# Attention and gated MLP on one core: weights loaded ahead of later mask rows and transposes, the second pair's VectorE work interleaved, the last output row in two column parts

## Chip, cores, metric

One core of one Trainium2 chip. The metric is the device time of one execution in microseconds (us); runs of a kernel before and after the change were taken on the same chip, in rounds.

## The reference

Bucketed attention (a query sees only keys of the same 6-bit hash bucket), then a gated MLP with a gated residual:

```python
q, k, v: (4, 8, 768, 64) fp32       # batch, heads, rows, head dim
proj: (64, 6); w_gate, w_val: (512, 1536); w_out: (1536, 512); w_res: (512, 512)

bucket(t) = sum_j 2^j * ((t @ proj)[..., j] > 0)
scores    = where(bucket(q) == bucket(k), q k^T / 8, -1e9)
attn      = softmax(scores) v                     # -> x: (3072, 512)
g         = x @ w_gate
ffn       = (gelu(g) * (x @ w_val)) @ w_out
out       = x + sigmoid(x @ w_res) * ffn          # fp32
```

## The kernel before

Heads are worked in pairs, 16 in all, four pairs to a batch. A pair is split into chunks, and every chunk is a **slot** of a schedule: its scores (TensorE), its exponential (ScalarE), the tasks that `at(slot, ...)` hung there, some matmuls of the MLP of the batch before, and the value matmuls of an earlier chunk. `base(p)` is the first slot of pair p; pair 0 has 12 slots, every later one 9. Four slots into a new batch the whole gate and value stage of the batch before is run (`gate_val`, 192 matmuls; no scores come in between, only the value matmuls that are still outstanding). In batch 0 there is no MLP to mix in.

In the traces here each engine takes its own instructions in program order (SyncE, SP, issues pair 5's load at 33.25 us, behind the two transposes hung ahead of it at 28.37). So the order in which tasks are hung is the order in which SP issues transfers and VectorE (DVE) makes copies. What the argument touches:

```python
    def load(p, what, ...):                 # q, k (sides 0, 1) or v (2) of pair p: nc.sync.dma_start
    def load_w():                           # 512 KB of a weight into one of NWS = 4 staging tiles, nc.sync
    def cast_w():                           # GpSimd: staging tile -> bf16 weight; frees the staging tile
    def transpose_dma(x):                   # nc.sync: nat -> aug
    def move_second(x):                     # GpSimd: rows 64..127 of aug -> second
    def mask_rows(p, engines):              # 4 small transfers: bucket rows into aug and second
    def blocks(x, ...):                     # DVE: 32x32 transposes of the raw load, for the hash
    def hash_half(p, dh, bank=(tp_ps, "tp")):
        ...
        for j, (x, c0, n) in enumerate(q4): # four column strips of TensorE, one for each operand
            nc.tensor.matmul(hs[32 * j:32 * j + 32], projw[:, dh, :],
                             t32[x][:, c0:c0 + n, dh, :], start=(dh == 0), stop=(dh == 1),
                             tile_position=(0, 32 * j), skip_group_check=True)
    # ... cut ...
    at(base(1) + 3, mask_rows, 2)
    for side in range(2):
        at(base(1) + 3, transpose_dma, (3, side))
    at(base(1) + 3, load, 3, (2,))
    at(base(1) + 4, load, 5, (0, 1))        # (cut: in program order behind the lines above)
    # ... cut ...
    for side in range(2):
        at(base(3) + 4, transpose_dma, (5, side))
    for i in range(NWS):
        at(base(2) + 1, load_w)             # first four weight loads
    # ... cut: load 5 (2,) ...
    at(base(3) + 4, load, 6, (0, 1))
    at(base(3) + 5, load, 7, (0, 1))
    # ... cut: load 6 (2,) ...
    for i in range(NWS):
        at(base(2) + 5 + i, cast_w)
        at(base(3) + 4, load_w)             # second four
        at(base(3) + 5 + i, cast_w)
    # ... cut: the end ...
    flush()                                 # the last value matmuls
    mlp_matmuls(HELD[-1])                   # HELD[-1] = 15 output matmuls kept for this place
    x_transpose(NPAIR - 1)
    gate_val(B - 1, flush)
    for _ in project(B - 1, ((row_ps, "row"), (av_ps, "av")), nc.vector):
        pass
```

## Time and profile before

| | before |
|---|---|
| median of its first three timed runs | 359.07 us (358.67 to 359.46) |
| the profiled run / its span on the core | 361.94 / 360.2 us |
| TensorE busy | 344.8 us of 360.2 |
| first matmul of the first gate stage | 55.81 us |
| first score after that stage | 89.97 us |

The profiled run is 2.9 us slower than the median of the timed ones. The lines of the profile stand in the prediction.

### The profile page before, as it was taken

How to read it: one execution, taken by the hardware profiler on the slowest of the kernel's cores; microseconds unless marked ns; L12 is line 12 of the kernel's file. 1: busy time of each engine (PE TensorE's matmuls, PEld its weight loads, DVE VectorE, ACT ScalarE, POOL GpSimd, SP SyncE). 2: the span in 40 equal slices, each digit the busy share in tenths (PEclk: the TensorE clock that was granted, in tenths of full speed). 3: DMA queues.
4: the chain of work that ended last, by engine and by line, in shares of the span. 5: the costliest groups of instructions: out<-in, count | busy, mean ns of one | idle time of the engine just before them, and what ended most of it. 6: DMA issues, size and time to landing. Idle time of an engine off the chain costs nothing.

```text
span 360.2 us, 7593 instructions
## 1 busy us (share of the span) xinstructions
PE 344.8 (96%) x3094; PEld 201.4 (56%) x3094; DVE 152.9 (42%) x229; ACT 211.7 (59%) x238; POOL 153.9 (43%) x194
## 2 busy tenths in 40 slices
PE   8899889799999999999999999999999999999994
PEld 4556366466465565566555566656555655666442
DVE  6884433243553346343452545434452024434243
ACT  5799696223778787323778788332778874232210
POOL 6696760976658579200048769300037222000000
PEclk9999999999999999999999999999999999999998
DMA  7748879999633583740002773510002220000012
GB/s 239 230 152 118 259 218 265 309 324 306 173 132 104 124 270 101 177 159 0 2 32 73 169 256 104 116 44 3 0 2 62 82 53 34 24 2 1 31 63 83
DMA packets 52574, 44.06 MB, mean 122 GB/s; under 512 B 31640, under 2 KB 44348, under 8 KB 52540
## 3 DMA queue, kind: packets, MB, share of 16 engines
q1 hardware_dynamic: 52396, 43.56, 41.9%
q8 instruction: 24, 0.39, 0.5%
q14 instruction: 10, 0.08, 0.1%
q0 software_dynamic: 64, 0.02, 0.0%
q10 hardware_dynamic: 80, 0.00, 0.0%
HBM read 29.36 MB, written 6.29 MB: 99 GB/s over the span
## 4 chain that ended last, share of the span: by engine, by line
PE 74%; POOL 10%; issue 5%; DMA 4%; DVE 3%; SPq 2%; ACT 1%; POOLq 0%; DVEq 0%; ACTq 0%
PE sp L457 31%; PE fps L487 15%; PE sp L435 11%; PE av L406 7%; PE rps L477 5%; PE hs L274 3%; POOL ldv L332 2%; POOL second L208 2%; DMA x_sb<-x_tok 2%; DMA ld<-in_k_dram 1%; POOL va L326 1%; SPq L203 1%; POOL wg L177 1%; POOL wv L177 1%; PE spr L287 1%
## 5 line engine op out<-in xcount | busy, mean ns | idle before, releaser
L439 ACT ACTIVATE e<-sp 128x1024 bf16<-128x1024 f32 (+1 forms) x147 | 144.7, 1007 | 33.9 <-PE sp L435 31.0
L463 ACT ACTIVATE gt<-sp 128x768 bf16<-128x768 f32 x48 | 38.9, 811 | 86.8 <-PE sp L457 86.8
L464 DVE SCALAR_TENSOR_TENSOR hh<-gt,sp 128x768 bf16<-128x768 bf16 x48 | 45.8, 954 | 83.8 <-PE sp L457 83.8
L487 PE MATMUL fps<-wo,hh 128*128 128x512 bf16 x288 | 76.4, 378 | 0.7 <-DVE o L492 0.7
L457 PE MATMUL sp<-x_sb,wg 128*128 128x512 bf16 (+1 forms) x384 | 71.1, 326 | 2.0 <-POOL wg L177 1.5
L457 PE MATMUL sp<-x_sb,wv 128*128 128x512 bf16 (+1 forms) x384 | 70.4, 326 | 0.3 <-POOL wv L177 0.3
L406 PEld LDWEIGHTS <-e 128*128 128x128 bf16 x1152 | 49.8, 97 | 31.8 <-issue 9.3
L406 PE MATMUL av<-va,e 128*128 128x65 bf16 x1152 | 56.1, 193 | 0.9 <-ACT e L439 0.7
L435 PE MATMUL sp<-aug,aug 71*128 71x512 bf16 x192 | 54.3, 326 | 1.9 <-ACT e L439 1.1
L435 PE MATMUL sp<-second,second 128*128 128x512 bf16 x192 | 54.3, 325 | 0.1
L457 PEld LDWEIGHTS <-wg 128*128 128x128 bf16 x384 | 37.3, 98 | 26.9 <-POOL wg L177 1.9
L457 PEld LDWEIGHTS <-wv 128*128 128x128 bf16 x384 | 37.4, 98 | 25.7 <-POOL wv L177 1.1
L494 POOL TENSOR_TENSOR o<-o,x_tok 128x512 f32<-128x512 f32 x18 | 20.8, 1156 | 56.1 <-DVE o L492 52.8
L487 PEld LDWEIGHTS <-hh 128*128 128x128 bf16 x288 | 27.6, 97 | 26.2
L383 POOL TENSOR_TENSOR x_tok<-total,rec 128x768 bf16<-128x768 f32 x9 | 13.3, 1473 | 49.2 <-DVE rec L382 49.2
L492 DVE SCALAR_TENSOR_TENSOR o<-th,fps 128x512 f32<-128x512 f32 x24 | 16.3, 681 | 39.5 <-PE fps L487 35.7
L208 POOL COPY second<-aug 64x768 bf16<-64x768 bf16 x30 | 24.4, 826 | 17.8 <-DMA aug<-nat 15.3
L237 DVE STREAM_TRANSPOSE t<-ld 128x768 f32<-128x768 f32 (+1 forms) x34 | 29.5, 907 | 2.7 <-DMA ld<-in_q_dram 2.3
L477 PE MATMUL rps<-wr,x_sb 128*128 128x512 bf16 x96 | 24.6, 379 | 0.0
L480 ACT ACTIVATE th<-rps 128x512 f32<-128x512 f32 x24 | 14.3, 596 | 17.4 <-PE rps L477 13.9
L435 PEld LDWEIGHTS <-second 128*128 128x128 bf16 x192 | 18.5, 98 | 5.1 <-issue 2.2
L294 DVE CAST bits<-spr 128x512 bf16<-128x512 f32 (+1 forms) x24 | 15.6, 656 | 8.9 <-PE spr L287 8.8
(67 smaller groups left out, 247.8 us busy)
## 6 DMA issues: line engine op xcount, KB each, us to landing
ldv<-in_v_dram SPq DMA_DIRECT2D x16, 384.0 KB
out_dram<-o SPq DMA_DIRECT2D x24, 256.0 KB
ld<-in_q_dram SPq DMA_DIRECT2D x15, 384.0 KB
ld<-in_k_dram SPq DMA_DIRECT2D x15, 384.0 KB
ws<-in_moe_w_gate_dram SPq DMA_DIRECT2D x6, 512.0 KB
ws<-in_moe_w_val_dram SPq DMA_DIRECT2D x6, 512.0 KB
ws<-in_moe_w_out_dram SPq DMA_DIRECT2D x6, 512.0 KB
ws<-in_moe_w_res_dram SPq DMA_DIRECT2D x2, 512.0 KB
```

The costliest lines, as they stand in the source:

```text
L208: eng.tensor_copy(second[x[0] % NM][x[1]][D:P], aug[x][D:P])
L237: nc.vector.transpose(t32[x][:, c0:c1].rearrange("p c h n -> p (c h n)"), raw[x][:, c0:c1].rearrange("p c d -> p (c d)"))
L406: nc.tensor.matmul(o[:, qt0 + i, :], e[:, off + i * P:off + (i + 1) * P], va[:, hi, jt, 0:D + 1], start=(hi not in begun), stop=(jt == T - ...
L435: nc.tensor.matmul(sp[:, off:off + nq * P], ks[0:n, jt, :], qs[0:n, qt0:qt0 + nq, :], start=True, stop=True)
L439: nc.scalar.activation(e[:, 0:n], sp[:, 0:n], AF.Exp, scale=float(ALPHA))
L457: nc.tensor.matmul(sp[:, c0:c1], w[:, kk, bass.ts(m, P)], xs[:, kk, c0:c1], start=(kk == 0), stop=(kk == KM - 1))
L463: nc.scalar.activation(gt, sp[:, 0:S], AF.Gelu)
L464: nc.vector.scalar_tensor_tensor(hh[:, m, :], gt, 0.5, ps[1][:, 0:S], op0=ALU.mult, op1=ALU.mult)
L477: nc.tensor.matmul(rps, x_sb[b][:, kk, t, :], wr[:, kk, :], start=(kk == 0), stop=(kk == KM - 1))
L487: nc.tensor.matmul(fps, hh[:, m, bass.ts(t, P)], wo[:, m, :], start=(m == 0), stop=(m == KF - 1))
L492: nc.vector.scalar_tensor_tensor(o, th, 1.0, fps, op0=ALU.add, op1=ALU.mult)
L494: last.tensor_add(o3, o3, x_tok[b][:, :, t, :])
```

## The change

It moves work; apart from twelve more matmuls, two more DVE steps and one more store in the last row, it neither adds nor drops any. Six parts, cut to their core:

```diff
 # 1 start
+    cast((0, 0), nc.scalar, H0)            # ahead of the copies of the projection
...
-    cast((0, 0), nc.scalar, H0)
-        at(1 + side, blocks, (1, side))
     at(2, spread_in_place, (0, 1), (ROW, TP))
+    at(2, blocks, (1, 0))
...  at(4 + side, transposed, (1, side), nc.vector)
+        if side == 0:
+            at(4, blocks, (1, 1))
-        at(4, hash_half, 1, dh, ROW)
+        at(5, hash_half, 1, dh, ROW)       # its first spread: slot 6 -> 7
-        at(7, blocks, (2, side))
+        at(6 + side, blocks, (2, side))
 # 2 load of pair 5
+    at(9, load, 5, (0, 1))
-    at(base(1) + 4, load, 5, (0, 1))
 # 3 second four weight loads now lead slot base(3)+4; behind them
+        at(base(3) + 5, transpose_dma, (5, side))      # was +4, ahead of them
+    at(base(3) + 6, load, 6, (0, 1))                   # was +4, ahead of them
+    at(base(3) + 7, load, 7, (0, 1))                   # was +5
+    at(base(3) + 7, load, 6, (2,))                     # was +6
+    at(base(3) + 8, ...) move_second 5, values_prep 5, mask_rows 5   # were +6, +6, +7
 # 4 seam
-    HELD = [0] + [12] * (B - 2) + [15]
+    HELD = [0] + [12] * (B - 2) + [19]
+    flush(1)
+    mlp_matmuls(4)
     flush()
 # 5 tail, in project(): the last row of the last batch in columns 0..383 and 384..511
+            parts = ((0, KM - 1), (KM - 1, KM)) if t == T - 1 and len(pools) > 1 else ((0, KM),)
+            for i, (k0, k1) in enumerate(parts):  # matmuls, DVE steps and store of each part
 # 6 mask rows of a later pair
-        at(s0 + 15, mask_rows, p + 1)
+        at(s0 + 16, mask_rows, p + 1)
```

The intent: the holes at the start, where the exponentials pace the kernel, are to close, the weights are to be there when the first gate stage wants them, and the last steps are to overlap.

More of the change, by code (lines that the diff above doesn't have):

```diff
@@ L483, in project @@
                 nc.sync.dma_start(*store)
-            ps, tag = pools[t % len(pools)]
-            fps = ps.tile([P, DMODEL], FP32, tag=tag, name="fps")
-            for m in range(KF):
-                nc.tensor.matmul(fps, hh[:, m, bass.ts(t, P)], wo[:, m, :],
-                                 start=(m == 0), stop=(m == KF - 1))
-                if m < KF - 1:
-                    yield 1
-            o = o_pool.tile([P, DMODEL], FP32, tag="o", name="o")
-            nc.vector.scalar_tensor_tensor(o, th, 1.0, fps, op0=ALU.add, op1=ALU.mult)
-            o3 = o.rearrange("p (k n) -> p k n", k=KM)
-            last.tensor_add(o3, o3, x_tok[b][:, :, t, :])
-            store = (out_t[b, t], o)
-            yield 1
+            o = o_pool.tile([P, DMODEL], FP32, tag="o", name="o")
+            parts = ((0, KM - 1), (KM - 1, KM)) if t == T - 1 and len(pools) > 1 else ((0, KM),)
+            for i, (k0, k1) in enumerate(parts):
+                cs = slice(k0 * P, k1 * P)
+                ps, tag = pools[(t + i) % len(pools)]
+                fps = ps.tile([P, (k1 - k0) * P], FP32, tag=tag, name="fps")
+                for m in range(KF):
+                    nc.tensor.matmul(fps, hh[:, m, bass.ts(t, P)], wo[:, m, cs],
+                                     start=(m == 0), stop=(m == KF - 1))
+                    if m < KF - 1:
+                        yield 1
+                if store and i:
+                    nc.sync.dma_start(*store)
+                nc.vector.scalar_tensor_tensor(o[:, cs], th[:, cs], 1.0, fps,
+                                               op0=ALU.add, op1=ALU.mult)
+                o3 = o[:, cs].rearrange("p (k n) -> p k n", k=k1 - k0)
+                last.tensor_add(o3, o3, x_tok[b][:, k0:k1, t, :])
+                store = (out_t[b, t][:, cs], o[:, cs])
+                yield 1
         nc.sync.dma_start(*store)
@@ L582 @@
     at(1, transposed_head, (0, 1), 1, nc.vector)
-    for side in range(2):
-        at(1 + side, blocks, (1, side))
     at(2, spread_in_place, (0, 1), (ROW, TP))
+    at(2, blocks, (1, 0))
     for side in range(2):
@@ L591 @@
         at(4 + side, transposed, (1, side), nc.vector)
+        if side == 0:
+            at(4, blocks, (1, 1))
         at(5 + side, move_second, (1, side))
     for dh in range(2):
-        at(4, hash_half, 1, dh, ROW)
-    at(6, spread, 1, 0, 4, ROW)
+        at(5, hash_half, 1, dh, ROW)
+    at(7, spread, 1, 0, 4, ROW)
     at(7, spread, 1, 4, T, TP)
@@ L630 @@
         at(base(1) + 7, cast, (5, side))
-        at(base(3) + 6, move_second, (5, side))
         for i in range(2):
@@ L637 @@
     at(base(3) + 3, mask_rows, 4)
-    at(base(3) + 7, mask_rows, 5)
     at(base(2) + 3, values_prep, 4)
-    at(base(3) + 6, values_prep, 5)
     at(base(2), load, 4, (2,))
@@ L643 @@
         at(base(2), transpose_dma, (4, side))
-        at(base(3) + 4, transpose_dma, (5, side))
         at(base(2) + 3, move_second, (4, side))
@@ L648 @@
     at(base(2) + 6, load, 5, (2,))
-    at(base(3) + 4, load, 6, (0, 1))
-    at(base(3) + 5, load, 7, (0, 1))
-    at(base(3) + 6, load, 6, (2,))
     for i in range(NWS):
@@ L655 @@
         at(base(3) + 5 + i, cast_w)
+    for side in range(2):
+        at(base(3) + 5, transpose_dma, (5, side))
+    at(base(3) + 6, load, 6, (0, 1))
+    at(base(3) + 7, load, 7, (0, 1))
+    at(base(3) + 7, load, 6, (2,))
+    for side in range(2):
+        at(base(3) + 8, move_second, (5, side))
+    at(base(3) + 8, values_prep, 5)
+    at(base(3) + 8, mask_rows, 5)
     for p in range(6, NPAIR, 2):
```

## The prediction

> **What bounds the kernel now.** I read the busy tenths first, then the stretches, then each engine in order of time where TensorE (PE) or ScalarE (ACT) stops, then the queue of SyncE (SP).
>
> ```profile
> PE   8899889799999999999999999999999999999994
> ACT  5799696223778787323778788332778874232210
> ```
>
> One slice is 9.0 us. PE is full from slice 9 on, up to the last slice. So only three places can give time: the start, up to about 71 us, the seam before the last gate stage (about 300 us), and the tail. The stretches say the same:
>
> ```profile
> 30.00:40.00 10.00, 7.92 (x104) 4.80 (x102) 5.76 (x8) 8.61 (x10) 4.95 (x10) 1.00 0.99 194
> 60.00:71.00 11.00, 9.29 (x56) 5.03 (x53) 3.00 (x4) 3.24 (x4) 8.27 (x10) 1.00 0.95 316
> 174.00:225.00 51.00, 51.00 (x542) 29.62 (x540) 23.67 (x35) 41.18 (x44) 32.03 (x37) 1.00 0.40 112
> ```
>
> Columns: length, then busy time of PE, weight loads, VectorE (DVE), ACT, GpSimd (POOL), granted clock, DMA share, GB/s. At 174 to 225 PE has no hole: nothing moved there is worth anything. Batch 0 has no matrix work of the second half to mix in, so there the exponentials set the pace (0.77 us each in pair 0, 0.95 us in the later pairs) and a hole in ACT is lost time. From 8.96 us on, ACT has these:
>
> ```profile
> 15.56 4.62 ACT L439 ACTIVATE e<-sp 128x768 bf16<-128x768 f32 x6 [1.73 <-PE sp L435]
> 41.94 1.02 ACT L439 ACTIVATE e<-sp 128x1024 bf16<-128x1024 f32 x1 [2.97 <-PE sp L435]
> ```
>
> Behind the second stands this chain on PE, DVE and SP:
>
> ```profile
> 38.64 0.85 PE L274 MATMUL hs<-t,projw 128*32 128x384 f32 x6 [0.86 <-DVE x_sb L393]
> 37.16 0.98 DVE L237 STREAM_TRANSPOSE t<-ld 128x768 f32<-128x768 f32 x1 [1.87 <-DMA ld<-in_q_dram]
> 38.84 0.98 DVE L237 STREAM_TRANSPOSE t<-ld 128x768 f32<-128x768 f32 x1 [0.26 <-DMA ld<-in_k_dram]
> 28.37 4.20 SPq L203 DMA_TRANSPOSE aug<-nat  x2
> 33.25 0.46 SPq L90 DMA_DIRECT2D ld<-in_q_dram  x1
> ```
>
> The load of pair 5 goes out at 33.25, behind mask rows and two transposes; its block transposes on DVE wait 1.87 us; the copy to x_sb stands behind them; the hash matmuls, which need that copy's buffer and those blocks, wait; the scores behind the hash wait; ACT starves.
>
> The weights come next. The gate stage starts at 55.81 and stalls at its fifth column block:
>
> ```profile
> 69.14 0.82 PE L457 MATMUL sp<-x_sb,wg 128*128 128x512 bf16 x4 [1.50 <-POOL wg L177]
> 70.12 0.82 PE L457 MATMUL sp<-x_sb,wv 128*128 128x512 bf16 x4 [0.16 <-POOL wv L177]
> 71.11 0.82 PE L457 MATMUL sp<-x_sb,wv 128*128 128x512 bf16 x4 [0.16 <-POOL wv L177]
> 62.37 1.04 POOL L177 CAST wg<-ws 128x1024 bf16<-128x1024 f32 x1 [11.12 <-DMA ws<-in_moe_w_gate_dram]
> ```
>
> POOL stood idle 11.12 us for weights that SP issued only at 55.77. At the seam and at the tail:
>
> ```profile
> 300.01 0.42 PE L406 MATMUL av<-va,e 128*128 128x65 bf16 x8 [0.69 <-ACT e L439]
> 355.67 0.69 DVE L492 SCALAR_TENSOR_TENSOR o<-th,fps 128x512 f32<-128x512 f32 x1 [2.04 <-PE fps L487]
> 356.39 0.69 DVE L494 TENSOR_TENSOR o<-o,x_tok 128x512 f32<-128x512 f32 x1
> ```
>
> **What the Trainium skill says.** "DMA: Bandwidth & Descriptors", section "Anatomy of one DMA — SWDGE (gpsimd) path", says that a semaphore wait happens on the issuing sequencer before dispatch, not in the DMA engines. So one waiting transfer holds all behind it on SP; the trace agrees (pair 5's load behind the 4.20 us of transposes). It also gives some 2 us fixed per DMA; the mask rows of 10.5 KB land 1.7 to 2.1 us after issue. "TensorE: Matmul & The Clock Gate", section "Architectural detail: the array is 16× 32×32, not 1× 128×128", calls VectorE and ScalarE strict FIFO and lets PE pull only weight loads ahead; the holes above show that in-order blocking. The same page, "Wait — 56ns, not 53.3ns?", gives N / 2.4 GHz + 2.5 ns per streamed matmul: 216 ns for 512 columns, and the chain of work has 12 of them in 2.59 us, 216 ns each.
>
> **The change part by part.**
>
> 1. Start. ACT casts the first query half before it copies the projection. The half is there at 3.35 (DVE reads it then), so the cast ends at about 3.9 instead of 4.73; but the warm-up holds PE until 4.58, so the transposes start 0.2 us earlier. Then DVE: the two mask copies of head (0,1) now come before pair 1's block transposes (1.84 us), and the second of these and the hash go to slots 4 and 5. I replayed the order with the measured durations: mask copies 10.8 to 11.9, blocks (1,0) to 12.8, copy out to 13.4, blocks (1,1) to 14.35, hash on PE 14.37 to 15.15, scores of slot 6 at 15.35. ACT: slot 5 ends at 14.4, slot 6 starts at 15.85, where before slot 6 started at 16.33. So the 1.73 us hole isn't closed but comes one exponential later and shrinks to some 1.4. Pair 1's mask rows leave at about 17.85 (17.71 before), land near 20.9, and hold its first scores about there: I count **-0.4 us**.
>
> 2. Pair 5's load moves from slot 16 to slot 9, right behind pair 4's (SP at about 21). It is in memory long before 35 us, so both DVE waits go (1.87 + 0.26) and x_sb is copied before the hash asks. What stays is the hash itself, 0.78 us a half on PE between scores, plus av 0.24: a hole of about 0.45 us. 2.97 - 0.45 = **-2.5 us**.
>
> 3. Weights. The second four loads move ahead of pair 5's transposes (2.57 us), of pair 6's and 7's loads, and of pair 5's mask rows. They need buffers that POOL's first casts free; POOL no longer waits 1.69 + 0.75 us for pair 5's cast, so I have these casts done at 49 (51.25 before), the loads out at 47 to 50 instead of 55.8 to 57.7, landed after the same 6.6 us (55.77 to 62.37) by 57, and cast by 58 to 61. The gate stage, then starting at about 52.9, needs them at about 63.5. The waits go: 1.50 + 0.16 + 0.16 = **-1.8 us**. The third four and the output weights follow by some 5 us earlier, so they don't become the wait.
>
> 4. Seam. HELD goes from 15 to 19: three more output matmuls and the four of the last gate row are kept and placed between the last two value steps, 7 x 0.216 = 1.5 us, over a hole of 0.69 us. The DVE chain after it (2.65 us from the end of av to x_tok) lies beside 12 matmuls (2.59 us) as before. **-0.7 us**.
>
> 5. Tail. 12 matmuls of 384 columns and 12 of 128: estimated from the skill's formula 12 x 162.5 + 12 x 55.8 ns = 2.62 us instead of 2.59. DVE: 0.69 us for 512 columns and 0.97 for 768 make about 0.13 + 0.0011 per column, so 0.55 for 384 and 0.27 for 128. First part ready at 354.95: DVE 355.03 to 356.16, then 0.27 + 0.27 and gaps to 356.75 instead of 357.08. The last store is 64 KB instead of 256 (about 1 us of traffic), worth some 0.3. **-0.6 us**.
>
> 6. The later mask rows (slot 15 to 16) and the blocks of pair 2 spread over two slots: nothing on the path, 0.
>
> Sum: 0.4 + 2.5 + 1.8 + 0.7 + 0.6 = 6.0. 359.07 - 6.0 = **353.1 us**. After 90 us PE is full, so what is gained before is carried through one to one.
>
> **Rivals.** (a) The weights become the bound: DMA ran at 316 GB/s and a share of 0.95 to 0.97 from 60 to 90 us, the last output weight is cast at 90.6 and read at about 93.9. Were they no earlier than now, a PE 4.7 us earlier would wait some 1.4 us there, and 0.5 at the third group: 355. Against it: at 50 to 52 us DMA moved 17 GB/s, a hole that the early loads fill. (b) The hole at 13 to 16 us closes fully: up to another 1.3 us, 351.8; or mask rows of pair 1, now behind a later hash, eat it: 353.5. (c) The hash remains a hole of a microsecond as it still shares one buffer with the transposes: 353.7 to 354. (d) The gap of the starved ACT only moves to pair 4's mask rows, issued up to 50.8 and read at 52.08, which had no slack: some 0.5 us back.
>
> **Range and chances.** The 2% line is 351.9, a gain of 7.2. It takes (b) in full. Losses from (a), (c) and (d) together would leave 356. I say 351.4 to 355.6; faster 0.20, within 2% 0.79, slower 0.01.
>
> **What would show it.** Right: ACT's hole near 39 to 42 about 0.5 us; gate stage from about 52.9; no wait of its matmuls on wg or wv; PE's first output rows near 85.3 instead of 90.4; no wait on wo; no 0.69 us wait at the seam; last DVE work 0.3 us sooner after PE's end. Wrong: a wait on POOL for weights after 70 us, the gate stage starting later than 54, or a new hole at PE after 90 us.

## The result, and the profile after

353.84 us median (353.09 to 355.25, four runs) against 359.26 (358.67 to 360.53, four runs): ratio 0.9849, 95% interval 0.9808 to 0.9890. Ratios here are the mean time of one kernel's runs over that of the other's runs of the same rounds, so not quite the ratio of the quoted medians. Predicted were 353.1, range 351.4 to 355.6.

Busy tenths after; a slice is 8.8 us, and TensorE (PE) is busy for 90% or more of every slice from the seventh on (from the ninth before):

```profile
PE   8999889999999999999999999999999999999995
ACT  5899895235787886323888788323778884232220
```

The stretches of 30 to 40 and 60 to 71 us after (length, then busy PE, weight loads, DVE, ACT, POOL, clock, DMA share, GB/s). PE went from 7.92 to 9.06 in the first and from 9.29 to 10.95 in the second:

```profile
30.00:40.00 10.00, 9.06 (x119) 5.30 (x120) 5.43 (x9) 9.05 (x10) 8.11 (x14) 1.00 0.76 149
60.00:71.00 11.00, 10.95 (x69) 6.62 (x68) 3.82 (x4) 3.66 (x5) 7.41 (x10) 1.00 1.02 362
```

ScalarE (ACT) in order of time; in brackets the idle time before the row and who ended it. The hole of 1.73 became 1.46 and comes one exponential later (three, not two, run before it); that of 2.97 became 0.82:

```profile
11.94 2.25 ACT L439 ACTIVATE e<-sp 128x768 bf16<-128x768 f32 x3
15.65 3.78 ACT L439 ACTIVATE e<-sp 128x768 bf16<-128x768 f32 x5 [1.46 <-PE sp L435]
38.99 1.02 ACT L439 ACTIVATE e<-sp 128x1024 bf16<-128x1024 f32 x1 [0.82 <-PE sp L435]
```

The chain behind the second hole, on SP, DVE and PE. Pair 5's load is out at 20.58 instead of 33.25, the block transposes wait for nothing, the hash (hs) runs as soon as PE comes to it. What is left of the hole is what PE does between two scores, the hash and the value matmuls:

```profile
20.58 0.47 SPq L90 DMA_DIRECT2D ld<-in_q_dram  x1
32.68 2.69 DVE L237 STREAM_TRANSPOSE t<-ld 128x768 f32<-128x768 f32 x3
36.92 0.85 PE L274 MATMUL hs<-t,projw 128*32 128x384 f32 x8
37.70 0.42 PE L406 MATMUL av<-va,e 128*128 128x65 bf16 x8
37.96 0.50 PE L413 MATMUL av<-vsum,eps_sb 128*128 128x390 bf16 x2
38.30 0.38 PE L435 MATMUL sp<-aug,aug 71*128 71x256 bf16 x2
```

The weights: POOL waits 3.21 us for them instead of 11.12, and casts at 51.99 instead of 62.37; the fifth column block of the gate stage has no wait:

```profile
51.99 1.04 POOL L177 CAST wg<-ws 128x1024 bf16<-128x1024 f32 x1 [3.21 <-DMA ws<-in_moe_w_gate_dram]
63.88 1.46 PE L457 MATMUL sp<-x_sb,wg 128*128 128x512 bf16 x8
```

The seam and the tail. The last value matmuls have no wait in front of them, and the last DVE step is 128 columns wide:

```profile
292.77 0.41 PE L406 MATMUL av<-va,e 128*128 128x65 bf16 x8
293.02 2.75 PE L492 MATMUL fps<-wo,hh 128*128 128x512 bf16 x12
347.78 0.55 DVE L498 SCALAR_TENSOR_TENSOR o<-th,fps 128x384 f32<-128x384 f32 x1 [1.40 <-PE fps L492]
349.16 0.29 DVE L501 TENSOR_TENSOR o<-o,x_tok 128x128 f32<-128x128 f32 x1
```

The two profiles set beside each other (starts on PE, but for the exponential, which is on ACT, and the last two rows):

| event | before | after | gained so far |
|---|---|---|---|
| first scores | 8.44 | 8.05 | 0.39 |
| first exponential of pair 1 | 21.84 | 21.11 | 0.73 |
| first matmul of gate stage 0 | 55.81 | 52.87 | 2.94 |
| first score behind it | 89.97 | 84.68 | 5.29 |
| first matmul behind gate stage 1 | 173.64 | 167.67 | 5.97 |
| first matmul of gate stage 3 | 303.50 | 296.24 | 7.26 |
| end of the last DVE step | 357.08 | 349.45 | 7.63 |
| span | 360.2 | 352.0 | 8.2 |

So the profiles say 8.2 us and the times 5.4. Profiling isn't the reason: the two profiled runs themselves took 361.94 and 353.80 us, 8.1 apart, and their spans are both 1.8 us shorter than these times. The profiled run of before was a slow one of its kind. What was slow in it is the question of the experiments, along with what each part is worth alone.

### The profile page after: what moved, and what is told of

The parts are those of the page before. It is cut to its first block, busy times and chain, and to the rows that moved or that the text cites.

```text
span 352.0 us, 7561 instructions
## 1 busy us (share of the span) xinstructions
PE 340.3 (97%) x3056; PEld 202.4 (57%) x3106; DVE 152.7 (43%) x231; ACT 211.3 (60%) x238; POOL 154.0 (44%) x194
## 4 chain that ended last, share of the span: by engine, by line
PE 89%; ACT 4%; DVE 4%; issue 2%; DVEq 0%; ACTq 0%
PE sp L457 35%; PE fps L492 16%; PE sp L435 15%; PE av L406 9%; PE rps L477 5%; PE hs L274 4%; ACT e L439 4%; PE spr L287 2%; DVE x_tok L383 1%; PE wps L182 1%; DVE o L498 1%; PE tp L392 1%; DVE total L376 1%; PE tp L217 0%; DVE bits L294 0%
## 5 line engine op out<-in xcount | busy, mean ns | idle before, releaser
L492 PE MATMUL fps<-wo,hh 128*128 128x512 bf16 (+2 forms) x284 | 73.1, 369 | 1.3 <-DVE o L498 0.3
L457 PE MATMUL sp<-x_sb,wg 128*128 128x256 bf16 (+1 forms) x378 | 70.4, 325 | 0.3
L435 PE MATMUL sp<-second,second 128*128 128x256 bf16 (+1 forms) x175 | 47.8, 320 | 0.2 <-ACT e L439 0.2
L498 DVE SCALAR_TENSOR_TENSOR o<-th,fps 128x512 f32<-128x512 f32 (+2 forms) x25 | 16.5, 659 | 42.1 <-PE fps L492 37.5
L435 PEld LDWEIGHTS <-aug 71*128 71x128 bf16 x192 | 16.4, 97 | 5.9 <-issue 1.7
```

Of the source, the lines that this page charges most:

```text
L435: nc.tensor.matmul(sp[:, off:off + nq * P], ks[0:n, jt, :], qs[0:n, qt0:qt0 + nq, :], start=True, stop=True)
L457: nc.tensor.matmul(sp[:, c0:c1], w[:, kk, bass.ts(m, P)], xs[:, kk, c0:c1], start=(kk == 0), stop=(kk == KM - 1))
L492: nc.tensor.matmul(fps, hh[:, m, bass.ts(t, P)], wo[:, m, cs], start=(m == 0), stop=(m == KF - 1))
L498: nc.vector.scalar_tensor_tensor(o[:, cs], th[:, cs], 1.0, fps, op0=ALU.add, op1=ALU.mult)
```

## Experiments

Main theory: the parts are worth what the prediction's steps say, they add up, and the first profile of before was a slow draw. Rivals: the weights take back what the start gives; mask rows or a transfer of x_tok set the pace somewhere; single parts count only together. All kernels gave correct results.

### The kernel before once more

No edit.

> The kernel before once more, unchanged, for a second profile of it. The first profile of before fell in a run of 361.94 us, 2.7 us above the median of its runs (359.26), and its span is 8.2 us longer than that of after, while the medians differ by 5.4. Theory A (the first profile is a slow draw: a wait on a transfer happened to be longer): this profile shows smaller PE waits on the weights at the fifth column block (2.3 us start to start in the first profile) or on x_sb before the second gate stage (0.7), and a span near 357.5. Rival B (profiling itself lengthens before more than after): all holes are as in the first profile and the span is again about 360. Time: ratio 1.000.

Measured: 360.44 us median, ratio 1.0038 (0.9995 to 1.0081); span 358.8. Keep that ratio in mind: it is the same program against itself, and it is about as far from 1 as the largest single part below. So a part's time can hardly be told from chance, and what it is worth is read from the traces. Theory A holds in its mechanism, for half of the size: the same program drew shorter waits. Gate stage 0 lasted 33.18 us instead of 34.16, ACT's hole near 40 us was 2.67 instead of 2.97, the wait on x_sb before gate stage 1 was 0.27 instead of 0.53 us recorded. PE at the fifth column block in this run:

```profile
67.61 0.82 PE L457 MATMUL sp<-x_sb,wg 128*128 128x512 bf16 x4 [0.53 <-POOL wg L177]
68.60 0.82 PE L457 MATMUL sp<-x_sb,wv 128*128 128x512 bf16 x4 [0.16 <-POOL wv L177]
69.58 0.82 PE L457 MATMUL sp<-x_sb,wv 128*128 128x512 bf16 x4 [0.16 <-POOL wv L177]
```

The first of these waits was 1.50 in the first profile. I had expected a span near 357.5; it is still above that, so the first profile's draw explains 1.4 of the 2.8 us between 8.2 and 5.4. The rest lies within the spread of the runs, but no wait was named for it: the timed runs of before lay between 357.51 and 361.56.

### Pair 5's load alone

```diff
+    at(9, load, 5, (0, 1))
-    at(base(1) + 4, load, 5, (0, 1))
```

> Before, with only the load of pair 5 moved from slot 16 to slot 9. Main theory: the ACT hole of 2.97 us near 39 to 42 becomes about 0.8 us, the first gate matmul comes 2.2 us earlier (53.6 instead of 55.8), time -2.2 us if the weights keep pace. Rival (the weights bound the gate stage): the gate starts earlier but stalls for weights by as much longer, since pair 6's and 7's loads and pair 5's transposes still go ahead of them; then the first score after the gate stage is at about 89.9 as before and the time is unchanged.

Measured: 358.01 us, ratio 0.9959 (0.9925 to 0.9993), so -1.5 us. ACT's hole is 0.82 us, as in after, and the gate stage starts 45.22 us after the first scores instead of 47.37 (47.09 in the second profile of before). Gate stage 0 still waits for weights and lasts 33.30 us, no longer than before (34.16 and 33.18); it doesn't stall by what was gained. The rival falls.

### The weights' order alone

```diff
     # slot base(3)+4: load_w x4 only; then, at +5 to +8:
+    transpose_dma 5, load 6, load 7, load 6 v, move_second 5, values_prep 5, mask_rows 5
```

> Before, with only the second four weight loads put ahead of pair 5's transposes, of pair 6's and 7's loads and of pair 5's mask rows. Main theory: the gate stage starts as before (about 55.8), has no wait on wg or wv, and lasts 31.8 instead of 34.2 us: time -2.3 us. Rival: the waits only move to the third four loads or to the output weights, as DMA is full from 55 to 90 us: gain under 1 us.

Measured: 357.97 us, ratio 0.9965 (0.9927 to 1.0003), -1.3 us, with no change still inside the interval. Gate stage 0 lasts 31.81 us, without a wait. The mechanism holds. The size of 2.3 was the first profile's draw: the seven profiles with the old order gave 34.16, 33.18, 33.30, 33.21, 32.46, 31.84 and 33.21 us (mean 33.05), the seven with the new one 31.81 or 31.82. So this part is worth 1.2 us on average, and takes a source of spread out. One run of the old order (31.84) had no wait at all.

### Mask rows one slot later, alone

```diff
-        at(s0 + 15, mask_rows, p + 1)
+        at(s0 + 16, mask_rows, p + 1)
```

> Before, with only the mask rows of the second pair of each two moved from slot 15 to slot 16 (a part that the prediction put at zero). Theory: the transposing transfer of x_tok into x_sb before the second gate stage no longer stands behind these mask rows in SP's queue; it goes out 2.5 us or more earlier, and the PE wait on x_sb (0.53 us recorded, 0.69 start to start) is gone: time -0.7 us. Rival (that wait went in the after kernel only because of other shifts): wait stays, time unchanged.

Measured: 359.74 us, ratio 1.0011 (0.9973 to 1.0048). The wait on x_sb was gone in this run, as the theory said, and no time was gained that the runs could show. A later run, after with slot 15, tests it from the other side.

### The start alone

```diff
 # part 1 of the change only
```

> Before, with only the changes at the start (query cast ahead of the projection copies on ACT; pair 1's block transposes behind the mask copies of head (0,1); hash of pair 1 in slot 5; blocks of pair 2 in slots 6 and 7). First transposes on PE at 4.5 instead of 4.75 to 4.79. From PE's first scores to the first exponential of pair 1: 13.40 us in both before profiles and about 13.0 here, so -0.3 to -0.4; ACT's first hole 1.46 instead of 1.73 and one exponential later. Time -0.6 us with 0.25 for the cast. Rival 1: pair 1's mask rows land no earlier, so nothing of the VectorE part is kept. Rival 2: the first scores come anywhere between 7.6 and 8.5 from run to run, whatever the order on ACT (the same six transposes last 0.52 or 0.85 us), so the cast's 0.25 us can't be seen in the time.

Measured: 358.64 us, ratio 0.9974 (0.9954 to 0.9994), -0.9 us. From the first scores to pair 1's first exponential 13.05 us against 13.40 in both profiles of before: -0.35, so rival 1 falls for this run. It isn't so in every run: the seven profiles with the new start (two of them with pair 1's hash one slot later still) give 13.02 to 13.06 in five and 13.36 and 13.40 in two, where pair 1's scores wait 0.51 and 0.72 us for their mask rows; the seven with the old start give 13.39 to 13.52 in six and 13.11 in one. The means are 13.14 and 13.37, -0.2. The first transposes start at 4.51 instead of 4.75 or 4.79. Rival 2 is right about the spread: the first scores came at 8.42 in this run, later than in after, and at 7.64 in a kernel with the old start. Two groups of six transposes on PE stand before them; here they are in the start kernel, and after them in the kernel with the late mask rows:

```profile
4.51 0.85 PE L217 MATMUL tp<-ident,nat 128*64 128x128 bf16 x6
6.09 0.85 PE L217 MATMUL tp<-ident,nat 128*64 128x128 bf16 x6
```

```profile
4.71 0.52 PE L217 MATMUL tp<-ident,nat 128*64 128x128 bf16 x6 [0.27 <-ACT nat L192]
5.63 0.52 PE L217 MATMUL tp<-ident,nat 128*64 128x128 bf16 x6
```

The same work took 0.85 or 0.52 us. The Trainium skill, "TensorE: Matmul & The Clock Gate", "Part 1: The HAM clock gate (the "warmup" mystery)", says that the array starts at half clock and that the moment at which it is released varies from run to run; the two durations fit that, though the profile's granted clock reads 1.00 there in both, so no run here shows it directly. So the cast's 0.25 us can't be told from the time. Over all 14 profiles the first scores start at 8.10 us on average with the old start and at 8.03 with the new.

### The seam alone

```diff
-    HELD = ... + [15]
+    HELD = ... + [19]
+    flush(1)
+    mlp_matmuls(4)
     flush()
```

> Before, with only the seam (HELD 15 to 19, and the matmuls between the last two value steps). Recorded PE waits before the last gate stage 0.69 (exponential) and 0.34 (output step of a row on DVE, near 290) vanish. Theory: each recorded PE wait costs some 0.16 us more than its column says, as the matmul ahead of it is drawn 0.16 us longer than its stream; so from the end of the third gate stage to the start of the fourth 47.67 us (before) becomes 46.38 (after's): -1.29. Rival (what the prediction said): only the 0.69 wait, -0.7. Time -1.3 or -0.7 us.

Measured: 358.01 us, ratio 0.9971 (0.9934 to 1.0008). The time leaves it open; the trace does not. From the end of gate stage 2 to the start of gate stage 3 there are 46.39 us, against 47.67 in the first profile of before and 47.68 in the tail kernel, which has the old seam: -1.29, the theory's figure, not the prediction's 0.7. Some profiles of both kinds are 0.4 to 0.7 us longer there, when a score near 270 us waits, mostly for mask rows; the means of seven and seven are 47.87 and 46.54, -1.3.

### The tail alone

```diff
 # part 5 of the change only
```

> Before, with only the last row in two column parts. Theory: from the start of the last row's output matmuls to the end of the last DVE step 3.88 us instead of 4.25 (-0.37), and from there to the end of the span 2.55 us instead of 3.12 as the last store is 64 KB: -0.9 us in all. Rival: the store's fixed part sets the end, so only the 0.37 counts.

Measured: 358.67 us, ratio 0.9980 (0.9961 to 0.9999), -0.7 us. From the start of the last row's output matmuls to the end of DVE 3.88 us instead of 4.26; from there to the end of the span 2.56 instead of 3.08. The theory holds, in both terms (-0.38 and -0.52), and the same lengths stand in every profile of either kind but the one with three parts.

### After, with the mask rows back at slot 15

```diff
-        at(s0 + 16, mask_rows, p + 1)
+        at(s0 + 15, mask_rows, p + 1)
```

> After, with only the mask rows of the second pair put back to slot 15. Theory: the transposing transfer into x_sb stands again behind them in SP's queue and the wait before the second gate stage comes back, 0.3 to 0.7 us (32.1 to 32.4 us for that stage instead of 31.7): after + 0.5 us, about 354.3. Rival: no wait, 353.8.

Measured: 354.49 us, ratio 0.9857 (0.9837 to 0.9878), within the interval of after. The transfer into x_sb goes out 4.56 us before gate stage 1 (131.75 to 136.31), against 7.09 in after (128.90 to 135.99), and yet the stage has no wait: 31.68 us. The rival holds for this run. Of the eight profiles with the mask rows at slot 15, two had the wait (32.37 and 32.12 us, both runs of before) and six did not (31.69 or 31.68); of the six with slot 16 none had it. The two are those in which the transfer went out latest before the stage, 4.29 and 4.31 us; the other six of slot 15 had 4.38 to 5.03 us, and slot 16 gives 7.07 to 7.29. So slot 15 leaves next to no slack, and slot 16 gives 2 to 3 us more. On the average of the eight that is worth 0.14 us, not 0.7, and the times of kernels can't show so little.

### After once more

No edit.

> After once more, for its span and its time on the chip of the next three. Theory (single parts add up: -0.41, -0.35, -0.26, -0.29, -0.20 and +0.11 per cent of the six runs make -1.4): ratio 0.985 to 0.987. The profile shows the same holes as the first of after (ACT 1.46, 0.82, 0.54, 0.61), no wait of the gate matmuls on weights; the first scores come anywhere from 7.6 to 8.5.

Measured: 354.38 us, ratio 0.9850 (0.9817 to 0.9883). The six single ratios give -0.26 -0.41 -0.35 +0.11 -0.29 -0.20 = -1.40%; after gave -1.51% and -1.50%. The parts add up as far as these intervals can tell: six of 0.2 to 0.4% make some 0.8% for the sum, or 2.8 us, if they are taken as independent. The traces are the closer check: each part's piece has the same length in after as alone (13.06 and 13.05 us to pair 1's first exponential, ACT's hole 0.82, gate stage 0 31.82, the stretch before gate stage 3 46.39, the tail 3.88 + 2.56), so no part is seen to need another. The holes are those of the first profile; the first scores came at 8.28.

### Pair 1's hash yet one slot later

```diff
-        at(5, hash_half, 1, dh, ROW)
+        at(6, hash_half, 1, dh, ROW)
```

> After, with pair 1's hash one slot later still (slot 6). Theory A (pair 1's first scores are held by its mask rows, whose copy stands behind the hash and is no earlier): ACT's hole of 1.46 us shrinks to about 0.7, but the time is given back before pair 1's first exponential, which stays about 13.0 us after the first scores; time as after. Rival B (the hole is worth its length): pair 1 starts 0.7 us sooner, time -0.7 us.

Measured: 354.18 us, ratio 0.9862 (0.9820 to 0.9903): as after. ACT in order of time shows where the hole went:

```profile
12.12 3.19 ACT L439 ACTIVATE e<-sp 128x768 bf16<-128x768 f32 x4
15.90 0.81 ACT L439 ACTIVATE e<-sp 128x768 bf16<-128x768 f32 x1 [0.59 <-PE sp L435]
16.93 2.25 ACT L439 ACTIVATE e<-sp 128x768 bf16<-128x768 f32 x3 [0.23 <-PE sp L435]
21.26 5.76 ACT L439 ACTIVATE e<-sp 128x1024 bf16<-128x1024 f32 x6 [0.88 <-PE sp L435]
```

1.46 became 0.59 + 0.23, but the hole before pair 1 grew from 0.60 to 0.88, and pair 1's first exponential comes 13.02 us after the first scores (13.06 in after). PE waits there for the mask rows:

```profile
20.57 0.38 PE L435 MATMUL sp<-aug,aug 71*128 71x512 bf16 x1 [0.35 <-DMA aug<-bits]
```

Theory A holds: in this run pair 1 is held by its mask rows, and what is gained ahead of them is given back there. In after itself the gap at this place is only 0.07 us, and the profile names no cause for it.

### Pair 4's hash in quarters (a miss)

```diff
-        at(base(2) + 7 + side, hash_half, 4, side)
+    for j in range(4):                       # one column strip j, both halves of the head dim
+        at(base(2) + 5 + j, hash_part, 4, j, ROW)
-        at(base(3) + s, spread, 4, 4 * i, 4 * i + 4)
+        at(base(3) + s, spread, 4, 4 * i, 4 * i + 4, ROW if i == 1 else TP)
```

> After, with the hash of pairs 4 and 5 cut into four quarters of 0.39 us in slots base(2)+5 to +8 and in the other accumulator, and its second spread in that one too. Theory: where the hash comes in two halves of 0.78 us, ACT starves 0.82 + 0.54 us, and the spread that waits for its buffer costs 0.61; with quarters PE needs 1.1 us a slot against ACT's 0.95, so some 0.8 us of holes remain of 1.97. Gate stage 1.0 to 1.2 us earlier against the first scores (44.82 to about 43.7), time -1.1 us. Rival: quarters need blocks that aren't there yet (pair 5's second at 36.7) and the holes only move: no change.

Measured: 357.15 us, ratio 0.9932 (0.9907 to 0.9956), 2.8 us worse than after. Neither theory: a quarter takes not 0.39 but 1.40 us (36.88 to 38.28), nearly twice a whole half:

```profile
36.88 1.48 PE L290 MATMUL hs<-t,projw 128*32 128x384 f32 x4
38.28 0.42 PE L422 MATMUL av<-va,e 128*128 128x65 bf16 x8
```

ACT then has holes of 0.95, 1.17, 1.51 and 1.17 us. A half sends its four matmuls (eight records in the trace, two for each) to four column strips, one after another, and they run beside each other: 8 records in 0.78 us. I had cut along the strips, so that both matmuls of a quarter (four records) wanted the same strip and followed one another. The Trainium skill, "TensorEngine Tiling (Array Packing)", "Key Properties", says that different tiles can execute in parallel; the trace agrees, 8 records in 0.78 us over four strips against 4 in 1.40 in one. A cut by columns, with all four strips in each quarter, wasn't run. The hole of 0.61 us isn't there in this profile; whether the other bank for the second spread or the moved hash removed it, this run can't tell.

### All three together

After with both edits above and the last row in three parts of 256, 128 and 128 columns:

```diff
-            parts = ((0, KM - 1), (KM - 1, KM)) if ...
+            parts = ((0, KM - 2), (KM - 2, KM - 1), (KM - 1, KM)) if ...
```

> After, with both of these and the last row in three column parts (256, 128, 128). Tail: last DVE step 0.4 us sooner after the start of the last row's matmuls (3.88 to 3.45). Sum by theory A: 1.1 + 0.4, ratio to before about 0.981; by B another 0.7.

Measured: 356.59 us, ratio 0.9916 (0.9885 to 0.9948). The quarters' loss is in it: ACT has their holes again, 0.96, 1.17, 1.52 and 1.17 us. The tail's part of the expectation held: from the start of the last row's matmuls to the end of DVE 3.52 us, against 3.88 in after. It was not run on its own. No kernel here is clearly faster than after.

## Why the prediction was right, and where not

The time fell inside the range, and the reading that batch 0's holes and the first weights' wait are where time can come from was right: both parts alone show it in the trace, and the gate stage started at 52.87 where 52.9 was said. That hit is partly luck: 0.39 of the 2.94 us gained there is the start of the first scores, which differs from run to run; counted from them the stage comes 2.56 us earlier. The sum of 6.0 came out as 5.4 (5.0 by the medians of the second measurement), with errors of both signs in the steps:

- **Step 1, start (-0.4):** by the trace -0.35 before pair 1 in five of seven profiles, -0.2 on average; by the time -0.9 (0.2 to 1.7). The cast's share isn't seen. Holes of 1.4 said, 1.46 found; that the mask rows hold pair 1, as said, is plain in three later profiles (waits of 0.35 to 0.72 us), not in after.
- **Step 2, pair 5's load (-2.5):** mechanism right, size wrong twice. The hole of 2.97 was the longest of seven draws (2.97, 2.67, 2.02, 2.25, 2.54, 2.41, 2.68, mean 2.51), and what is left is 0.82, not 0.45: beside the hash and the eight value matmuls I forgot the two matmuls of the value sums, 0.34 us of PE. 2.51 - 0.82 = 1.7; the time said 1.5. One reading beside it was wrong: the 4.20 us of transposes ahead of the load are drawn as SP at work, not as a transfer that waits. What waited in that queue was the first of pair 2's mask rows, 4.3 us for its bits, up to 25.23; the load stood behind all of it.
- **Step 3, weights (-1.8):** mechanism right, the size was right for the wrong reason. I summed recorded waits, 1.82; start to start the first profile had lost 2.35 (34.16 against 31.81), but it was a slow draw, and the mean loss is 1.2. The casts ran from 51.99 to 58.54, earlier than the 58 to 61 said: the first of these loads was there 4.06 us after its issue, not 6.6. Rival (a) fell: in after the last output weight is cast at 83.09 to 84.13 and no output matmul waits for a weight.
- **Step 4, seam (-0.7):** mis-sized by half. It took one wait of 0.69 and left out one of 0.34 just ahead, which also goes since the held matmuls change the order there; and each recorded wait costs 0.16 us more than its bracket. 0.69 + 0.34 + 2 x 0.16 = 1.35, against 1.29 measured.
- **Step 5, tail (-0.6):** 0.38 for DVE (0.33 said) and 0.52 for the smaller store (0.3 said): 0.90.
- **Step 6 (0):** right within what the times can show. It overlooked a wait: the first profile has one of 0.53 us on x_sb in gate stage 1, 0.69 start to start, which is the step from 5.29 to 5.97 in the table. "PE is full after 90 us" wasn't quite so; on average the wait is worth 0.14 us.
- **Base:** lengths of holes came from a run of 361.94 us and were taken off a median of 359.07. That error and the short terms of the seam and tail nearly cancel. The total was good in part by luck; the places and causes were not luck. With the lengths of all 14 profiles the terms are 0.2 to 0.35, 1.7, 1.2, 1.3 and 0.9: 5.3 to 5.5 us, against 5.4 and 5.0 by the times.

Of the other rivals, (b) in its winning form didn't come: the hole stayed, and where a later run halved it, no time followed. In its losing form it is what holds pair 1. (c) came nearly true in size, 0.82 us, but not for its reason: in after no hash matmul waits for the buffer. (d) is a draw too: pair 4's first scores wait 0.20 to 0.26 us in twelve profiles, with and without the change, and 0.49 and 0.83 in one of each, where the profile names the mask rows.

## What to carry to other kernels

Before you subtract a hole from a time, look at a second profile of the same kernel: waits that ended with a transfer were draws here (31.84 to 34.16 us for one stage), and the worth of removing one is its mean; it also stops varying (31.81 or 31.82 in seven profiles). And before you trust a part's time, measure the old kernel against itself: here that came out 0.4% off, about as much as the largest part. An in-order issue queue is a schedule: a transfer that nobody waits for yet (mask rows, transposes of a later pair) can cost another engine microseconds by standing ahead of a load (ACT's hole of 2.51 us on average became 0.82). And when you cut a group of small matmuls into pieces to spread them over slots, don't cut it along what runs side by side; that the other cut would have helped wasn't run.

## What the Trainium skill lacked or had wrong

- No page that I read says how a recorded wait of TensorE relates to the time lost, though the latency of one matmul and its spacing in a stream are given. Here matmuls of 512 columns are drawn as 0.38 us and stream in 0.216, so each bracketed wait stands for 0.16 us more: 1.50 + 0.16 + 0.16 recorded make 2.30, and 2.35 were lost. It would belong to "TensorE: Matmul & The Clock Gate", whose per-matmul 216 ns the traces confirm.
- "DMA: Bandwidth & Descriptors" gives fixed and variable parts of a transfer but I found no spread for one and the same program. With the old order the gate stage that waits for the weights lasted 31.84 to 34.16 us in seven runs.
- "TensorEngine Tiling (Array Packing)" tells the gain of using tiles side by side, not the price of using one in a row: 1.40 us for a quarter of the hash in one strip, 0.78 for a half over four.
